# One-token attention with an MLP beside it: cache tiles of four heads on one load queue, folds on TensorE, and weights in the cache buffers

## Chip, cores, metric

The kernel runs on one core of one Trainium2 chip. The metric is the device time of one execution in microseconds, as the median of several executions. Where two kernels are compared by a ratio, it is the mean time of one kernel's fast runs over the mean time of the other's in the same rounds on the same chip, so it is not quite the ratio of the medians beside it.

## The reference

Eight requests each decode one token: a layer norm, attention of 32 heads over a cache of 4096 keys, and an MLP of the doubly normalised input; the sum of both and the input goes out.

```python
B, Sq, D = 8, 1, 576;  H, Sk, Dh = 32, 4096, 128;  F = 4608      # all bf16

q = (x @ wq).reshape(B, Sq, H, Dh).transpose(0, 2, 1, 3)
scores = einsum("bhqd,bhkd->bhqk", q, k_cache) * (Dh ** -0.5)
o = einsum("bhqk,bhkd->bhqd", softmax(scores), v_cache)
A = o.transpose(0, 2, 1, 3).reshape(B, Sq, H * Dh) @ wo

h = gelu(layernorm(x) @ w1 + b1)          # B_ref, x is already normalised once
out = x0 + A + h @ w2 + b2
```

The two caches are 268 MB each; every byte of them is read once and meets one multiply-add. The weights are 20 MB.

## The kernel before

The program is laid out in stages, each with its own memory pools: the query projection, then the MLP, then the attention loop, then the output projection. A pool that is closed gives its memory to the next one, so the cache buffers (`kv_pool`) partly lie where the MLP's weights lay.

```python
    wo_sb = const.tile([P, H, D], BF16, name="wo_sb")
    nc.gpsimd.dma_start(out=wo_sb, in_=A_wo.rearrange("(h p) d -> p h d", p=P))
    ...                                   # wq, layer norms, q8 = queries, qT = their transposes
    with tc.tile_pool(name="mlp_w", bufs=1) as mlp_w, ...:
        w1_sb = mlp_w.tile([P, NDC, F], BF16, name="w1_sb")        # 46 KB a partition
        w2_sb = mlp_w.tile([P, FC, D], BF16, name="w2_sb")         # 41 KB a partition
        b1T = mlp_w.tile([P, FC], BF16, name="b1T")
        nc.gpsimd.dma_start(out=b1T, in_=B_b1.rearrange("(c p) -> p c", p=P))
        ...                               # the whole MLP
```

The loop takes two heads of one request at a time. A head's 4096 keys lie as 128 partitions of 32 keys, 8 KB of contiguous memory each. K comes on the queue of SyncE and V on that of ScalarE, three buffers each. Twelve of the 32 key columns are transposed and scored on TensorE; the other 20 are multiplied by the broadcast query on VectorE and folded there from 128 products to 8 by a tree of additions. The values are 64 matmuls with a single moving column each.

```python
        for b in range(B):
            for hg in range(NHG):
                nc.sync.dma_start(
                    out=k_sb, in_=A_k_cache[b, h0:h0 + HG].rearrange("g (p c) d -> p g c d", p=P))
                nc.scalar.dma_start(
                    out=v_sb, in_=A_v_cache[b, h0:h0 + HG].rearrange("g (p c) d -> p g c d", p=P))
                ...
                        nc.tensor.matmul(tp[:, t * P:(t + 1) * P], lhsT=k_sb[:, g, c, :], rhs=ident[:, :], ...)
                        nc.scalar.activation(out=kT[:, g, blk, :], in_=tp[:, :], func=ACT.Copy)
                ...
                        nc.tensor.matmul(sc_ps[:, g, c:c + 1], lhsT=kT[...], rhs=qT[:, h, b:b + 1], ...)
                ...
                        nc.vector.tensor_tensor(out=prod[:, g, :, :], in0=k_sb[:, g, X:C, :], in1=qb_cur[...], op=ALU.mult)
                        while width > 8:  # 128 -> 64 -> 32 -> 16 -> 8
                            nc.vector.tensor_tensor(out=prod[:, g, :, 0:half], in0=..., in1=..., op=ALU.add)
                        nc.vector.tensor_reduce(out=sc_ps[:, g, X:C], in_=prod[:, g, :, 0:width], ...)
                ...
                    nc.scalar.activation(out=E[:, g, :], in_=sc_ps[:, g, :], func=ACT.Exp, accum_out=...)
                ...
                    for c in range(C):
                        nc.tensor.matmul(o_ps[:, g:g + 1], lhsT=v_sb[:, g, c, :], rhs=E[:, g, c:c + 1], ...)
```

The softmax here doesn't subtract the row's maximum and nothing guards it: scores larger than these inputs give would overflow.

## Time and profile before

| | before |
|---|---|
| median time, 13 runs | 1392.74 us (1391.15 to 1395.41) |
| span of the profiled run | 1389.7 us |
| first K load issued | 85.83 us |
| last K tile read | 1361.15 us |
| cache stream in between | 1275.3 us, 536.9 MB, 421 GB/s |
| mean rate over the span | 401 GB/s |
| TensorE's granted clock, mean | 0.52 |
| instructions | 33564 |

The lines of the profile are shown in the prediction. To read them: the rows of digits are 40 equal slices of the span, a digit being the busy share in tenths; `PEclk` is the clock that TensorE was granted, in tenths of full speed; `DMA` is the share for which the 16 DMA engines moved packets. A line of busy times by stage has the stretch, its length, busy time and number of instructions of PE, PEld, VectorE, ScalarE and POOL (PE is TensorE's matmuls, PEld its weight loads, POOL is GpSimd; SPq and ACTq, further down, are the queues of SyncE and ScalarE that issue loads), then granted clock, DMA share and GB/s. The question put to such a profile is which resource is full, when, and what happens in the slices where it is not.

### The profile page before, as it was taken

The page shows a single profiled execution, that of the slowest core. Times are in us where ns is not written, and L with a number is a line of the kernel's source. Part 1 is how long each engine was busy: PE and PEld are TensorE (multiplying, and loading weights), DVE is VectorE, ACT ScalarE, POOL GpSimd, SP SyncE. Part 2 cuts the span into 40 slices and gives each one's busy share as a digit, 9 for nine tenths or more (in the row PEclk, how much of TensorE's full clock was granted, in tenths as well). Part 3 has the DMA queues.
Part 4 walks back from the last instruction along what each step waited for, and adds up shares of the span by engine and source line. Part 5 has one row for each costly group of instructions (what it writes and reads, how often), then busy time and mean ns, then how long its engine had stood idle before and what let it go on. Part 6 is the DMA issues. An engine that isn't in the chain of part 4 may idle for free.

```text
span 1389.7 us, 33564 instructions
## 1 busy us (share of the span) xinstructions
PE 800.5 (58%) x14800; PEld 670.2 (48%) x14800; DVE 850.2 (61%) x1604; ACT 551.4 (40%) x1485; POOL 9.6 (1%) x17
## 2 busy tenths in 40 slices
PE   4645565746565556565556555655556555556566
PEld 1324454545454545454545454555445545445454
DVE  2026666666666676666675766666766666666663
ACT  2213343534344434443444443443435443434342
POOL 1100000000000000000000000000000000000000
PEclk9565555555555555555555555555555555555556
DMA  7859999999999999999999999999999999999991
GB/s 273 306 203 427 425 426 426 426 426 426 426 424 424 424 419 426 420 426 426 416 425 426 413 427 419 425 425 418 425 423 419 425 421 427 424 415 426 417 425 69
DMA packets 73458, 559.12 MB, mean 402 GB/s; under 512 B 4424, under 2 KB 4448, under 8 KB 6624
## 3 DMA queue, kind: packets, MB, share of 16 engines
q10 hardware_dynamic: 35472, 273.16, 47.2%
q1 hardware_dynamic: 34848, 268.46, 45.8%
q0 software_dynamic: 2992, 15.35, 3.1%
q8 instruction: 115, 1.88, 0.5%
q14 instruction: 31, 0.25, 0.0%
HBM read 556.95 MB, written 0.01 MB: 401 GB/s over the span
## 4 chain that ended last, share of the span: by engine, by line
DMA 63%; DVE 21%; PE 11%; ACT 3%; issue 1%; ACTq 1%; POOL 0%; DVEq 0%; SPq 0%
DMA k_sb<-in_A_k_cache_dram 60%; DVE prod L287 9%; DVE prod L278 9%; PE o_ps L308 6%; DMA b1T<-in_B_b_dram 2%; PE tp L260 2%; DVE sc_ps L294 2%; ACT kT L264 2%; DMA wq_sb<-in_A_wq_dram 1%; ACT E L302 1%; PE qps L142 1%; PE acc L336 1%; PE mlp_ps L200 1%; ACTq L242 1%; ACT O_sb L312 0%
## 5 line engine op out<-in xcount | busy, mean ns | idle before, releaser
L278 DVE TENSOR_TENSOR prod<-k_sb,qb_sb 128x2560 bf16<-128x2560 bf16 x256 | 370.4, 1489 | 444.9 <-DMA k_sb<-in_A_k_cache_dram 444.9
L308 PE MATMUL o_ps<-E,v_sb 128*128 128x1 bf16 x8192 | 236.3, 165 | 463.7 <-ACT E L302 463.7
L264 ACT ACTIVATE kT<-tp 128x512 bf16<-128x512 f32 x768 | 442.5, 596 | 117.2 <-PE tp L260 85.1
L308 PEld LDWEIGHTS <-v_sb 128*128 128x128 bf16 x8192 | 243.2, 105 | 488.7 <-issue 488.7
L260 PE MATMUL tp<-ident,k_sb 128*128 128x128 bf16 x3072 | 440.7, 302 | 63.7 <-ACT kT L264 31.8
L287 DVE TENSOR_TENSOR prod<-prod 128x1280 bf16<-128x1280 bf16 (+3 forms) x1024 | 401.4, 466 | 0.1
L260 PEld LDWEIGHTS <-k_sb 128*128 128x128 bf16 x3072 | 291.6, 130 | 99.2 <-issue 59.6
L302 ACT ACTIVATE E<-sc_ps 128x32 bf16<-128x32 f32 x256 | 48.1, 193 | 474.4 <-DVE sc_ps L294 474.4
L269 PEld LDWEIGHTS <-kT 128*128 128x128 bf16 x3072 | 171.0, 116 | 53.2 <-ACT kT L264 53.1
L269 PE MATMUL sc_ps<-qT,kT 128*128 128x1 bf16 x3072 | 173.0, 172 | 5.1 <-ACT kT L264 0.2
L294 DVE TENSOR_REDUCE sc_ps<-prod 128x20 f32<-128x160 bf16 x256 | 83.4, 326 | 6.1 <-PE sc_ps L269 1.7
L312 ACT ACTIVATE O_sb<-o_ps 128x2 f32<-128x2 f32 x128 | 22.3, 174 | 156.9 <-PE o_ps L308 156.9
L228 PE MATMUL qb_ps<-q,sel 8*128 8x512 bf16 x64 | 37.3, 583 | 20.7 <-ACT qb_sb L229 20.6
L229 ACT ACTIVATE qb_sb<-qb_ps 128x512 bf16<-128x512 f32 x64 | 38.4, 599 | 26.3 <-DVE prod L278 16.0
L302 ACT ACTIVATION_READ_ACCUMULATOR E<-sc_ps 128x1 f32 x256 | 47.7, 198 | 0.0
L142 PE MATMUL qps<-wq_sb,xT 128*8 128x512 bf16 (+1 forms) x40 | 13.9, 457 | 11.0 <-DMA wq_sb<-in_A_wq_dram 11.0
L179 DVE TENSOR_TENSOR x<-hT_ps,b1T 128x288 f32<-128x288 f32 x1 | 0.5, 458 | 29.1 <-DMA b1T<-in_B_b_dram 29.1
L200 PE MATMUL mlp_ps<-w_sb,hT_sb 128*8 128x512 bf16 x72 | 10.3, 309 | 10.2 <-DVE hT_sb L190 10.2
L172 PEld LDWEIGHTS <-w_sb 128*128 128x128 bf16 (+1 forms) x180 | 10.6, 106 | 6.6 <-issue 5.4
L150 DVE CAST qT<-tq 128x8 bf16<-128x8 f32 x32 | 4.1, 162 | 14.2 <-PE tq L149 14.0
L146 ACT ACTIVATE q<-qps 8x512 bf16<-8x512 f32 x8 | 4.7, 587 | 20.2 <-PE qps L142 20.2
L172 PE MATMUL hT_ps<-yT,w_sb 128*128 128x8 bf16 (+1 forms) x180 | 12.0, 176 | 0.3 <-DVE qT L150 0.3
(56 smaller groups left out, 65.5 us busy)
## 6 DMA issues: line engine op xcount, KB each, us to landing
k_sb<-in_A_k_cache_dram SPq DMA_DIRECT2D x128, 2048.0 KB, 18.9
v_sb<-in_A_v_cache_dram ACTq DMA_DIRECT2D x128, 2048.0 KB, 17.1
w_sb<-in_B_w_dram POOLq DMA_DIRECT2D x1, 5184.0 KB, 30.8
wo_sb<-in_A_wo_dram POOLq DMA_DIRECT2D x1, 4608.0 KB, 26.9
w_sb<-in_B_w_dram POOLq DMA_DIRECT2D x4, 1152.0 KB, 9.0
wq_sb<-in_A_wq_dram ACTq DMA_DIRECT2D x4, 1024.0 KB, 9.7
w_sb<-in_B_w_dram POOLq DMA_DIRECT2D x1, 576.0 KB, 17.3
wq_sb<-in_A_wq_dram ACTq DMA_DIRECT2D x1, 512.0 KB, 18.0
```

What stands on the lines that cost most here:

```text
L142: nc.tensor.matmul(qps[:, :nn], lhsT=xT[:dn, ci, :], rhs=wq_sb[:dn, ci, n0:n0 + nn], start=(ci == 0), stop=(ci == NDC - 1),)
L200: nc.tensor.matmul(mlp_ps2[:, n0:n0 + nn], lhsT=hT_sb[:, fc, :], rhs=w2_sb[:, fc, n0:n0 + nn], start=(fc == 0), stop=(fc == FC - 1),)
L228: nc.tensor.matmul(qb_ps[:, :nn], lhsT=sel[:, b, :], rhs=q8[:, n0:n0 + nn], start=True, stop=True)
L229: nc.scalar.activation(out=qb_sb[:, n0:n0 + nn], in_=qb_ps[:, :nn], func=ACT.Copy)
L260: nc.tensor.matmul(tp[:, t * P:(t + 1) * P], lhsT=k_sb[:, g, c, :], rhs=ident[:, :], start=True, stop=True,)
L264: nc.scalar.activation(out=kT[:, g, blk, :], in_=tp[:, :], func=ACT.Copy)
L269: nc.tensor.matmul(sc_ps[:, g, c:c + 1], lhsT=kT[:, g, blk, t * P:(t + 1) * P], rhs=qT[:, h, b:b + 1], start=True, stop=True,)
L278: nc.vector.tensor_tensor(out=prod[:, g, :, :], in0=k_sb[:, g, X:C, :], in1=qb_cur[:, h * Dh:(h + 1) * Dh].unsqueeze(1).to_broadcast([P, R ...
L287: nc.vector.tensor_tensor(out=prod[:, g, :, 0:half], in0=prod[:, g, :, 0:half], in1=prod[:, g, :, half:width], op=ALU.add,)
L294: nc.vector.tensor_reduce(out=sc_ps[:, g, X:C], in_=prod[:, g, :, 0:width], axis=mybir.AxisListType.X, op=ALU.add,)
L302: nc.scalar.activation(out=E[:, g, :], in_=sc_ps[:, g, :], func=ACT.Exp, accum_out=Epart[:, h, b:b + 1],)
L308: nc.tensor.matmul(o_ps[:, g:g + 1], lhsT=v_sb[:, g, c, :], rhs=E[:, g, c:c + 1], start=(c == 0), stop=(c == C - 1),)
```

## The change

The intent is to let the transfer of the caches run from the first microseconds to the last and to keep all compute behind it. Tiles hold four heads of one request, 32 partitions a head, so each partition takes 32 KB of contiguous memory. All loads go on SyncE's queue through four buffers of 32 KB a partition; wq and w1 use these buffers before the stream, wo and w2 after it. VectorE multiplies all keys, TensorE folds the products against an identity matrix, and the values are matmuls of 512 moving columns. The order of all engines is fixed by hand. The core of the diff, cut:

```diff
+    ctx.enter_context(tc.manual_schedule(
+        engines={ENG.PE, ENG.DVE, ENG.Activation, ENG.SP, ENG.Pool}))
     const = ctx.enter_context(tc.tile_pool(name="const", bufs=1))
+    kv = ctx.enter_context(tc.tile_pool(name="kv", bufs=4))
...
+    wq_sb = kv.tile([P, WN * 2, HQ], BF16, name="wq_a", tag="kv")
+    wq_sb2 = kv.tile([P, WN, HQ], BF16, name="wq_b", tag="kv")
...
+    w1_sb = kv.tile([P, WN * 2, HF], BF16, name="w1_a", tag="kv")
+    w1_sb2 = kv.tile([P, WN, HF], BF16, name="w1_b", tag="kv")
...
+    def load_kv(cache, hg, b, name):
+        t = kv.tile([P, C, Dh], BF16, name=name, tag="kv")
+        nc.sync.dma_start(
+            out=t[:].rearrange("p c d -> p (c d)"),
+            in_=cache[b, hg * G:(hg + 1) * G].rearrange("g (p c) d -> (g p) (c d)", p=QP),
+        )
+        return t
...
-                nc.sync.dma_start(
-                    out=k_sb, in_=A_k_cache[b, h0:h0 + HG].rearrange("g (p c) d -> p g c d", p=P)
-                )
-                nc.scalar.dma_start(
-                    out=v_sb, in_=A_v_cache[b, h0:h0 + HG].rearrange("g (p c) d -> p g c d", p=P)
-                )
...
+        for n in range(NCB):
+            prod = prp.tile([P, CB, Dh], BF16, name="prod", tag="prod")
+            nc.vector.tensor_tensor(
+                out=prod, in0=k[:, n * CB:(n + 1) * CB, :],
+                in1=qb[:, v, b, h2].unsqueeze(1).to_broadcast([P, CB, Dh]), op=ALU.mult)
+            ps = ps_s.tile([P, CB, DL], FP32, name="s_ps", tag="s")
+            nd = Dh // DL
+            for d in range(nd):
                 nc.tensor.matmul(
...
+                    ps, lhsT=ident, rhs=prod[:, :, d * DL:(d + 1) * DL],
+                    start=(d == 0), stop=(d == nd - 1))
...
+        for j in range(J):
+            nc.tensor.matmul(
+                ps, lhsT=e[:, j], rhs=v[:, 4 * j:4 * j + 4, :], start=(j == 0), stop=(j == J - 1))
...
+        sc = scores(i, k_t)
+        if pend is not None:
+            gather(*pend)
...
+            softmax_last(i, sc)
+            values_last(i, v_t)
...
+    cuts = [(0, 0, R), (1, 0, R // 2), (1, R // 2, R - 3), (1, R - 3, R)]
+    for v, r0, r1 in cuts:
+        nc.sync.dma_start(out=w2_sb[v][:, r0:r1, :], in_=w2_v[v, :, r0:r1, :])
...
-        fin = fin_sb.tile([B, D], BF16, name="fin")
-        nc.vector.tensor_tensor(out=fin, in0=acc, in1=mlpx_sb, op=ALU.add)
+    fin = const.tile([B, D], BF16, name="fin")
+    nc.vector.tensor_copy(out=fin, in_=acc[:, :D])
```

## The prediction

> **What bounds the kernel now.** I read the page's slices first, then the chain of waits, the busy times by stage, the waits of the DMA-issuing queue, and the timeline of the end.
>
> The slices show a core whose DMA engines are full in 36 of 40 slices, at about 425 GB/s, while no compute engine is above seven tenths in the middle. The clock line says that TensorE is granted half of its speed almost throughout.
>
> ```profile
> span 1389.7 us, 33564 instructions
> DVE  2026666666666676666675766666766666666663
> PEclk9565555555555555555555555555555555555556
> DMA  7859999999999999999999999999999999999991
> GB/s 273 306 203 427 425 426 426 426 426 426 426 424 424 424 419 426 420 426 426 416 425 426 413 427 419 425 425 418 425 423 419 425 421 427 424 415 426 417 425 69
> q8 instruction: 115, 1.88, 0.5%
> HBM read 556.95 MB, written 0.01 MB: 401 GB/s over the span
> DMA k_sb<-in_A_k_cache_dram 60%; DVE prod L287 9%; DVE prod L278 9%; PE o_ps L308 6%; DMA b1T<-in_B_b_dram 2%; PE tp L260 2%; DVE sc_ps L294 2%; ACT kT L264 2%; DMA wq_sb<-in_A_wq_dram 1%; ACT E L302 1%; PE qps L142 1%; PE acc L336 1%; PE mlp_ps L200 1%; ACTq L242 1%; ACT O_sb L312 0%
> ```
>
> The chain runs through VectorE work for 20%, but that is a path through a loaded pipe, not the bound: the busy times by stage (busy time and count per engine, clock, DMA share, GB/s) have the DMA share at 1.01 over the whole cache stream and under it only at the two ends.
>
> ```profile
> 30.00:40.00 10.00, 7.75 (x46) 3.48 (x46) 3.42 (x27) 5.22 (x9) 6.54 (x8) 0.82 0.52 191
> 60.00:80.00 20.00, 9.83 (x104) 6.28 (x104) 3.02 (x7) 0.44 (x1) 0.00 (x0) 0.57 0.21 67
> 100.00:1350.00 1250.00, 723.46 (x14046) 627.43 (x14044) 817.59 (x1509) 522.05 (x1423) 0.00 (x0) 0.50 1.01 423
> 1360.00:1370.00 10.00, 7.67 (x145) 6.75 (x143) 7.00 (x14) 5.78 (x15) 0.00 (x0) 0.50 0.14 57
> 1370.00:1380.00 10.00, 6.78 (x83) 3.73 (x83) 2.42 (x3) 0.64 (x5) 0.00 (x0) 0.50 0.01 2
> ```
>
> What holds the first K load back shows in the waits of the issuing queue and in the timeline, where that load is issued only at 85.83 us; the last K tile is read at 1361.15 us and the output projection closes the run.
>
> ```profile
> SPq L239 <- DMA w_sb<-in_B_w_dram: 65.8, 1, 65.8
> SPq L239 <- DVE mlpx_sb L206: 15.1, 1, 15.1
> 85.83 1.42 SPq L239 DMA_DIRECT2D k_sb<-in_A_k_cache_dram  x3
> 1361.15 1.49 DVE L278 TENSOR_TENSOR prod<-k_sb,qb_sb 128x2560 bf16<-128x2560 bf16 x1 [3.30 <-DMA k_sb<-in_A_k_cache_dram]
> 1376.13 10.50 PE L336 MATMUL acc<-wo_sb,On 128*8 128x512 bf16 x64 [2.53 <-DVE On L326]
> ```
>
> So the span is 85.8 us of setup, 1275.3 us of stream and 28.6 us of tail. The caches are 2 x 8 x 32 x 4096 x 128 x 2 bytes = 536.9 MB, which makes the stream 421 GB/s. The four weight matrices are 20.1 MB, or 47 us at 425 GB/s: the setup spends about 39 us more on them than their bytes need, because the cache buffers wait for the MLP to finish, and the tail has an idle DMA.
>
> **What the Trainium skill says.** "DMA: Bandwidth & Descriptors", section "Bandwidth", gives 425 GB/s for a 16 MB load by one core and a ceiling of 435.2 GB/s. The trace agrees: 426 to 427 in the clean slices. The section "Issuing engines are not separate DMA queues" says that several issuing engines save only issue time; this case's trace has two queues in the stream and cannot confirm it, and the change relies on it. "TensorE: Matmul & The Clock Gate", Part 1, says that a dense stream of some 4 us doubles the clock. The trace agrees at the end of the run: the output projection's pairs of 512 and 64 columns come every 0.48 us until 1381.3 us, then 21 pairs take 5.02 us, 0.239 us each. That is 0.83 and 0.415 ns a column. "SBUF — State Buffer", section "Door 1: The DMA port swizzle", gives SBUF lines of 16 bytes and full bandwidth within one. No operand of the kernel before is read by TensorE in strided runs of 16 bytes, so the trace does not test it.
>
> **The change, part by part.**
>
> Setup. It removes the pool that made the caches wait for the MLP. The weights wq (4.72 MB) and w1 (5.31 MB) now sit in the same four buffers of 32 KB a partition as the cache tiles; wo and w2 move to the end. Ten MB at 425 GB/s are 23.6 us, from about 2 us on: the weights have landed at about 26 us. To follow without a gap, K of tile 0 needs the first wq buffer free by then. The normalised input is ready at 6.8 us in the trace; 18 tiny copies, one wide copy, nine transposes and two masks are added, so I estimate its spread form at 13 us. The first 24 query matmuls then take 24 x about 0.25 us (the trace's dense query groups: five in 1.26 us at full clock), so the buffer is free at 19 us. V follows. K of tile 1 needs the first w1 buffer; the 162 hidden matmuls of 16 columns cost 0.11 us each by the trace's weight loads (106 ns), 18 us after about 24 us, and the buffer frees near 36 to 40 us, before the 45.7 us at which tile 0 has landed. I see no gap. First cache byte at 26 us instead of 86.
>
> Stream. A tile is now 4 heads with 32 rows each, 4.19 MB of K and as much of V: 64 tiles, 19.7 us each at 426 GB/s. Rows are 32 KB of contiguous memory instead of 8 KB, all on one queue. VectorE loses the add tree and keeps two multiplies of 8192 elements and two reductions of 512. The slope between 1280 and 2560 elements is (1489 - 819)/1280 = 0.523 ns for one, so a multiply is 1489 + 5632 x 0.523 = 4.44 us; with some 0.7 us a reduction, 10.3 us a tile. TensorE loses the transposes and gets 32 matmuls against the identity that fold 128 products to 8, and 32 for the values, each 512 columns: 32768 x 0.415 = 13.6 us at full clock, 27.3 us at half. ScalarE has four exponentials at about 0.4 us with their accumulator reads and two small copies. K is released after its two multiplies, 8.9 us after it lands; its buffer is wanted again 29.5 us after landing. V is released about 4.4 + 7 + 4 + 7 = 22.5 us after K has landed, which is 12.7 us after its own landing, and has 29.5 us too. At full clock all of it hides behind the transfer. Executed TensorE instructions fall to a third, which should remove most of the 1.88 MB of instruction fetches.
>
> Rate. The pace of clean stretches in the trace (multiply starts at 603.95, 613.71 and 623.55 us: 9.8 us for 4.19 MB) is 428 GB/s and the mean 421; every 95 us or so a stretch of 10 to 20 us falls to between 391 and 415. I take 426 for the new kernel, since there is less fetching and rows are longer: 536.9 MB / 426 = 1260 us.
>
> Tail. After the last V byte come wo in 1152-byte rows (estimate 350 GB/s, 13.5 us) and w2 in long rows (12.5 us). The last tile's values are computed meanwhile: 128 narrow matmuls at 29 ns, since 64 of these took 1.85 us before, done some 10.5 us after V. 68 pairs of 512 and 64 columns at 0.24 us are 16 us and follow the weights; after the last piece only three pairs remain. Receipt 2, pairs 0.8, copy 0.7, output 2.4 us: the tail is about 32 us, a little longer than before, but it now carries 10 MB.
>
> Sum: 2 + 23.6 + 1260 + 32 = 1317.6 us of span. The measured times lie 1.8 to 3.4 us above the span; with the small chance of a better rate I say 1317 us, 5.5% less than 1393.
>
> **Rivals.**
> First, TensorE becomes the bound. At half clock it needs 27.3 us a tile: 64 x 27.3 + 60 gives 1800 us. For it: the clock line is 5 although TensorE was busy 58%. Against it: those matmuls had 1 or 128 columns; the new ones are dense, and a TensorE that falls behind has no idle time left and so warms, as the end of this trace shows. A milder form: the 16-byte strided reads run at half rate, 32 x 0.213 = 6.8 us more, 20.4 us a tile plus 1 us of gathers; then 64 x 21.5 + 60 = 1436 us, slower. I give both together 5%.
> Second, one queue with four large buffers does not keep 16 engines full; a hole of 1 us a tile costs 64 us and leaves 1380 us, the same. Against it: two to four loads should be pending at any time by the release times above. 4%.
> Third, the stream keeps its mean of 421 GB/s because the dips are not instruction fetches: 1275 us of stream, 1333 in all. 20%.
> Fourth, long rows bring it to 431 GB/s: 1246 us, 1303 in all. 20%.
> Fifth, the setup has a gap because a weight buffer frees late: each late microsecond adds one; I allow 10 us, 1327.
>
> **Range and chances.** The third and the fourth rival with a few microseconds at the ends give 1302 to 1336 us. Under 1365 us is faster by over 2%: 0.93. Within 2%: 0.03, a hole in the queue. Slower: 0.04, TensorE.
>
> **What would show each step.** Right: DMA share at 1.0 from the second slice to the last but one, first K issue before 26 us, PEclk at 8 or more in most slices, multiplies near 4.44 us, matmuls of both kinds spaced some 0.21 us, fewer packets on q8, a tail of some 32 us with full DMA for 25 of them. Wrong: VectorE no longer waiting for K but for TensorE (TensorE is the bound); GB/s with regular holes while the issuing queue waits on a matmul or multiply (late release); 421 GB/s with the same dips although q8 is small (the dips are something else).

## The result

The changed kernel took 1311.16 us in the median of 8 runs (1311.02 to 1312.0), against 1392.74 us before. The ratio is 0.9416, with a 95% interval from 0.9407 to 0.9426: 5.8% less.

The page of the kernel after, the lines that answer to those of before:

```profile
span 1309.3 us, 11800 instructions
DVE  2645545545545545544554554654654553654550
PEclk9799999999989999999998999989998989989998
DMA  9999999999999999999999999999999999999997
GB/s 402 431 430 430 431 430 431 431 432 430 431 432 432 431 431 431 431 430 430 431 429 431 430 432 432 432 432 432 431 429 431 430 431 432 429 431 432 430 418 274
q8 instruction: 40, 0.66, 0.2%
HBM read 556.94 MB, written 0.01 MB: 425 GB/s over the span
DMA k<-in_A_k_cache_dram 73%; DVE prod L281 21%; PE acc L268 1%; PE qps L213 1%; PE hT_ps L242 1%; PE s_ps L287 0%; PE o_last L329 0%; ACT e_last L321 0%; DMA prod<-in_A_x_dram 0%; DVE prod L181 0%; PE tp L185 0%; ACT L156 0%; DVE par L177 0%; DVE prod L158 0%; ACT q L220 0%
```

The `DMA` row is nine in 39 of 40 slices. The holes of the first three slices are gone, and the plateau stands at 429 to 432 GB/s where it was 413 to 427. VectorE is at half, and the digit of TensorE's clock is 9 or 8 in all slices but one.

The busy times by stage of the kernel after, with the columns as explained above:

```profile
0.00:10.00 10.00, 0.47 (x8) 0.47 (x9) 4.90 (x27) 1.58 (x2) 3.75 (x15) 1.00 0.81 314
10.00:20.00 10.00, 6.69 (x33) 2.86 (x33) 3.60 (x13) 0.29 (x1) 0.00 (x0) 1.00 1.01 432
20.00:30.00 10.00, 9.28 (x102) 6.26 (x101) 1.28 (x2) 3.44 (x5) 0.00 (x0) 0.89 1.06 452
100.00:1250.00 1150.00, 965.23 (x4309) 419.68 (x4308) 595.77 (x251) 144.73 (x602) 0.00 (x0) 0.94 1.00 431
1290.00:1300.00 10.00, 10.00 (x78) 4.65 (x76) 0.66 (x2) 0.00 (x0) 0.00 (x0) 0.96 0.92 384
1300.00:1310.00 10.00, 6.33 (x52) 2.90 (x50) 0.75 (x1) 0.00 (x0) 0.00 (x0) 1.00 0.13 50
```

And its timeline at the two ends (start, duration, engine, line, operation):

```profile
21.22 0.33 SPq L125 DMA_DIRECT2D k<-in_A_k_cache_dram  x1
...
32.44 0.33 SPq L125 DMA_DIRECT2D k<-in_A_k_cache_dram  x1
...
1268.24 8.76 DVE L281 TENSOR_TENSOR prod<-k,qb 128x8192 bf16<-128x8192 bf16 x2 [6.28 <-DMA k<-in_A_k_cache_dram]
...
1284.00 3.56 PE L329 MATMUL o_last<-e_last,v 128*128 128x4 bf16 x128 [2.35 <-ACT e_last L321]
...
1297.35 8.98 PE L268 MATMUL acc<-w,hT_sb 128*8 128x512 bf16 x72
1306.37 0.75 DVE L408 CAST fin<-acc 8x576 bf16<-8x576 f32 x1 [12.07 <-PE acc L268]
```

The load of the first cache tile is issued while w1 is still on its way, so the transfer never pauses: the first 10.0 MB, the weights, have passed after 26.0 us (314, 432 and 452 GB/s in the first three stretches of 10 us). The last V load was issued at 1251.8 us; the median landing of a V load is 24.7 us after issue, so it landed at about 1276.5 us. The span divides like this:

| | before | after | difference | predicted difference |
|---|---|---|---|---|
| setup, until the caches move | 85.8 us | 26.0 us | -59.8 | -60.2 |
| cache stream | 1275.3 us | 1250.5 us | -24.8 | -15.3 |
| tail | 28.6 us | 32.8 us | +4.2 | +3.4 |
| span | 1389.7 us | 1309.3 us | -80.4 | -72.1 |

The stream after is 536.9 MB in 1250.5 us, or 429 GB/s. Its first and last microseconds are read from cumulated rates and a median landing, so they are good to 1 or 2 us. The stream before is counted to the last K tile read, at 1361.15 us; the line from 1360 us on in the prediction (57 GB/s for 10 us, 0.6 MB) shows that the V loads had then ended too, so the two streams compare.

### The profile page after: what moved, and what is told of

Same layout as the page of the kernel before. It is cut to its first block, busy times and chain, and to the rows that moved or that the text cites. A ratio compares the mean times of both kernels' runs of the same rounds, so it can differ in the third digit from the quotient of the medians.

```text
span 1309.3 us, 11800 instructions
## 1 busy us (share of the span) xinstructions
PE 1085.0 (83%) x5150; PEld 480.2 (37%) x5150; DVE 661.9 (51%) x321; ACT 163.0 (12%) x662; POOL 3.7 (0%) x15
## 2 busy tenths in 40 slices
DMA packets 24089, 557.71 MB, mean 426 GB/s; under 512 B 2259, under 2 KB 6372, under 8 KB 6630
## 4 chain that ended last, share of the span: by engine, by line
DMA 74%; DVE 22%; PE 3%; ACT 0%; issue 0%; DVEq 0%; ACTq 0%
DMA k<-in_A_k_cache_dram 73%; DVE prod L281 21%; PE acc L268 1%; PE qps L213 1%; PE hT_ps L242 1%; PE s_ps L287 0%; PE o_last L329 0%; ACT e_last L321 0%; DMA prod<-in_A_x_dram 0%; DVE prod L181 0%; PE tp L185 0%; ACT L156 0%; DVE par L177 0%; DVE prod L158 0%; ACT q L220 0%
## 5 line engine op out<-in xcount | busy, mean ns | idle before, releaser
L281 DVE TENSOR_TENSOR prod<-k,qb 128x8192 bf16<-128x8192 bf16 x128 | 560.7, 4422 | 387.5 <-DMA k<-in_A_k_cache_dram 387.5
L308 PE MATMUL o_ps<-v,ebd 128*16 128x512 bf16 x2016 | 507.1, 416 | 118.2 <-ACT ebd L300 118.2
L287 PE MATMUL s_ps<-prod,ident 128*128 128x512 bf16 x2048 | 465.4, 381 | 87.2 <-DVE prod L281 87.0
L308 PEld LDWEIGHTS <-ebd 128*16 128x16 bf16 x2016 | 189.5, 96 | 410.3 <-ACT ebd L300 124.3
L287 PEld LDWEIGHTS <-ident 128*128 128x128 bf16 x2048 | 198.1, 98 | 349.9 <-issue 131.7
L292 DVE TENSOR_REDUCE sc<-s_ps 128x64 f32<-128x512 f32 x128 | 88.1, 689 | 200.3 <-PE s_ps L287 200.3
L300 ACT ACTIVATE ebd<-sc 32x128 bf16<-32x128 f32 x252 | 77.3, 307 | 17.9 <-DVE sc L292 14.9
L337 PEld LDWEIGHTS oT<-selc,ob 16*128 16x128 f32 x504 | 60.7, 186 | 26.7 <-issue 26.7
L337 PE MATMUL oT<-selc,ob 16*128 16x4 f32 x504 | 66.2, 250 | 0.0
L300 ACT ACTIVATION_READ_ACCUMULATOR ebd<-sc 32x1 f32 x252 | 46.3, 184 | 0.0
## 6 DMA issues: line engine op xcount, KB each, us to landing
v<-in_A_v_cache_dram SPq DMA_DIRECT2D x64, 4096.0 KB, 24.7
```

The costliest lines, as they stand in the source:

```text
L281: nc.vector.tensor_tensor(out=prod, in0=k[:, n * CB:(n + 1) * CB, :], in1=qb[:, v, b, h2].unsqueeze(1).to_broadcast([P, CB, Dh]), op=ALU.mult)
L287: nc.tensor.matmul(ps, lhsT=ident, rhs=prod[:, :, d * DL:(d + 1) * DL], start=(d == 0), stop=(d == nd - 1))
L292: nc.vector.tensor_reduce(out=sc[:, n * CB:(n + 1) * CB], in_=ps, axis=AX.X, op=ALU.add)
L300: nc.scalar.activation(out=e[rows, :, g, :], in_=sc[rows, :].rearrange("p (j c) -> p j c", c=4), func=ACT.Exp, scale=scale, accum_out=Ep[r ...
L308: nc.tensor.matmul(ps, lhsT=e[:, j], rhs=v[:, 4 * j:4 * j + 4, :], start=(j == 0), stop=(j == J - 1))
L337: nc.tensor.matmul(ps, lhsT=ob[:, c, :], rhs=selc[:, c, :], start=(c == 0), stop=(c == 3))
```

## Experiments

Three questions were put to the chip. What made the stream faster than 426 GB/s: longer rows, fewer instructions to fetch, or one queue in place of two? How near is TensorE to being the bound? And can the ends be improved?

### 8 KB pieces in place of 32 KB rows (rows8k)

```diff
-        t = kv.tile([P, C, Dh], BF16, name=name, tag="kv")
+        t = kv.tile([P, U, n + 16], BF16, name=name, tag="kv")     # U = 4, n = 4096 elements
         nc.sync.dma_start(
-            out=t[:].rearrange("p c d -> p (c d)"), ...
+            out=t[:, :, 0:n], ...
```

The 16 spare elements (32 bytes) after each piece keep the transfer from being one run of 32 KB. Nothing else differs but the views by which the tile is read.

> The changed kernel with one thing undone: each cache tile still comes in one load on one queue, but its rows land in four pieces of 8 KB with a gap of 32 bytes between them, so each transfer moves 8 KB as in the kernel before and not 32 KB. Theory of row length (a fixed cost per packet, worked out as about 4.4 ns from clean stretches at 427.3 GB/s with 8 KB and 432.0 GB/s with 32 KB): the clean rate falls to 427 GB/s, the time rises by 13 to 15 us to about 1325 us, with some 65 thousand more packets... of 8 KB for the caches. Theory that only instruction fetches or the number of queues made the stream faster: no change, 1311 us within 2.

Measured: 1335.48 us, ratio to before 0.9589 (0.9573 to 0.9605), 24.3 us more than the changed kernel. The page counts 73241 packets in place of 24089, that is 49152 more (the expectation's number was wrong). The busy times of its stream:

```profile
100.00:1250.00 1150.00, 952.50 (x4226) 414.19 (x4225) 585.99 (x246) 142.35 (x592) 0.00 (x0) 0.94 1.01 423
```

The stream fell from 431 to 423 GB/s with the same instructions on the same queue, so the shape of the transfer does matter, and more than expected: 24.3 us for 3072 more packets on each of the 16 DMA engines are 7.9 ns a packet. It also fell below the 426 GB/s that 8 KB packets had in the clean slices of the kernel before, which row length alone cannot explain.

### 2 KB pieces (rows2k)

The same edit with U = 16.

> The same with sixteen pieces of 2 KB a row. Row length with 4.4 ns a packet: 75.6 + 4.4 = 80.0 ns for 2 KB on one of 16 engines, 410 GB/s, some 67 us more, about 1379 us. If short rows cost more than a fixed time per packet, still slower; if row length is without effect, 1311 us.

Measured: 1434.74 us, ratio 1.0302 (1.0286 to 1.0317). This is slower than the kernel before.

```profile
100.00:1250.00 1150.00, 897.48 (x3915) 387.45 (x3914) 546.07 (x226) 131.17 (x543) 0.00 (x0) 0.93 1.05 392
```

123.6 us more for 15360 more packets an engine are 8.0 ns a packet, about the same as with 8 KB. So the cost goes with the number of packets, as the theory says, but it is nearly twice the 4.4 ns that were worked out from two kernels that differ in more than row length. The later runs show that two costs are in it. Note the DMA share: 1.05 while it moves 392 GB/s. A share of 1 does not say that bytes move at the best rate.

### The bias load moved to the front of the kernel before (before_b1early)

```diff
-        b1T = mlp_w.tile([P, FC], BF16, name="b1T")
-        nc.gpsimd.dma_start(out=b1T, in_=B_b1.rearrange("(c p) -> p c", p=P))
...
+    b1T = const.tile([P, FC], BF16, name="b1T")
+    nc.gpsimd.dma_start(out=b1T, in_=B_b1.rearrange("(c p) -> p c", p=P))
     wo_sb = const.tile([P, H, D], BF16, name="wo_sb")
```

> The kernel before with its first-layer bias load (4608 single elements of 2 bytes, which landed 32 us after its issue and ended the wait of the MLP) moved to the start of the program, ahead of the weights. The MLP then waits for its second weight matrix alone (landed at about 67 us in place of the bias at 70 us, or sooner without the small packets in front): the first cache load is issued 3 to 15 us earlier and the time falls by as much, to between 1378 and 1390 us. If the bias was not what held the MLP: 1393 us.

Measured: 1405.78 us, 14.6 us slower than before (ratio 1.0101, 1.0085 to 1.0116): a miss. Its timeline and busy times:

```profile
82.84 16.18 SPq L239 DMA_DIRECT2D k_sb<-in_A_k_cache_dram  x4
```

```profile
100.00:1350.00 1250.00, 714.22 (x13845) 619.16 (x13846) 806.41 (x1487) 514.97 (x1403) 0.00 (x0) 0.50 1.01 418
```

The setup did what was expected of it, at the low end: the first cache load left at 82.84 in place of 85.83 us. But the stream, whose code was not touched, ran at 418 in place of 423 GB/s. What did move were the addresses. The built programs tell where each buffer starts in its partition: in the kernel before, K and V buffers start on multiples of 256 bytes (72960, 122112, ...); the small bias tile ahead of them shifted all by 96 bytes (73056, 122208, ...). The buffers of the changed kernel start 96 bytes past a multiple of 256 too (48736, 147040, ...). "DMA: Bandwidth & Descriptors" of the Trainium skill, section "How a descriptor splits into AXI transactions", says that a descriptor which does not start on 256 bytes has a first transaction from the boundary below, whose unused bytes still cost beats. That gave the next two runs. They change the other kernel; no run repeats the early bias with its buffers back on a multiple of 256, so for this run the cause is argued from them.

### The changed kernel with its buffers moved by 160 bytes (aligned)

```diff
     const = ctx.enter_context(tc.tile_pool(name="const", bufs=1))
+    align = const.tile([P, 80], BF16, name="align")                # never used
```

> The changed kernel with 160 unused bytes ahead of its buffers, nothing else. As built, its cache buffers start 96 bytes past a multiple of 256 in each partition, while those of the kernel before start on a multiple; moving the buffers of the kernel before by 96 bytes (which the run with the early bias did as a side effect) went with a stream of 418 in place of 423 GB/s. If the start matters by a fixed time per packet (2.4 to 4.6 ns, estimated from 8 KB packets at 420, 423 and 426 GB/s), 1024 packets per engine make 2.5 to 4.7 us: 1306.5 to 1309 us, faster than both kernels. If the early bias slowed its stream by something else: 1311 us.

Measured: 1306.37 us (1306.21 to 1306.97), ratio 0.9383 (0.937 to 0.9396): 4.8 us less than the changed kernel, whose interval begins at 0.9407. It beats both kernels.

```profile
100.00:1250.00 1150.00, 976.09 (x4328) 422.77 (x4327) 600.30 (x252) 145.21 (x603) 0.00 (x0) 0.94 1.00 433
```

The buffers' start in SBUF (the on-chip memory) is worth 2 GB/s with 32 KB packets: 4.8 us over 1024 packets an engine are 4.7 ns each.

### 8 KB pieces, each on a multiple of 256 bytes (rows8k_al)

The edit of the first experiment with 128 spare elements in place of 16, and the 160 bytes in front.

> The run with 8 KB pieces again, now with every piece starting on a multiple of 256 bytes (gaps of 256 in place of 32 bytes). If the start matters: the stream returns to about the 426 GB/s that 8 KB packets had in the kernel before, 1324 to 1328 us, and what remains over 1311 is row length. If it does not: 1335 us as with the gaps of 32 bytes. If row length were nothing but alignment: 1311 us or less.

Measured: 1321.34 us, ratio 0.9489 (0.9476 to 0.9502).

```profile
100.00:1250.00 1150.00, 962.23 (x4273) 417.80 (x4272) 594.03 (x249) 142.86 (x593) 0.00 (x0) 0.94 1.01 428
```

Here both causes come apart. Between the two aligned kernels, 32 KB and 8 KB packets differ by 15.0 us, 4.9 ns for each further packet on an engine: row length. Between the two kernels with 8 KB pieces the start differs by 14.1 us, 3.5 ns for each of 4096 packets on an engine: alignment. (With gaps of 32 bytes one piece in eight starts on a multiple of 256 by chance, so this is a mean over all.) The 7.9 ns of rows8k hold both; for 2 KB pieces no run takes them apart. Nor was any multiple but 256 tried: whether 64 or 128 bytes would do, and whether the page's extra transaction is the mechanism, stays open. The changed kernel won about 15 us by its rows and gave 4.8 us back by where its buffers start.

### One queue for the kernel before (before_oneq)

```diff
-                nc.scalar.dma_start(
+                nc.sync.dma_start(
                     out=v_sb, in_=A_v_cache[b, h0:h0 + HG].rearrange("g (p c) d -> p g c d", p=P)
```

> The kernel before with its V loads issued from SyncE as well, so that one queue carries the stream; nothing else is changed. If one queue in place of two was part of the gain: the stream speeds up by up to 10 us, 1383 us. If it is row length and instruction fetches: 1393 us within 3.

Measured: 1387.63 us, ratio 0.9976 (0.9959 to 0.9993), 3.5 us less than the 1391.18 us of before in the same rounds. The theory of queues allowed up to 10 us; the other one expected no more than 3 us either way, and the measurement lies just outside, with an interval (1.0 to 5.7 us by the ratio) that reaches into both. The slices decide more than the time. Its page, and the busy times of its stream:

```profile
GB/s 273 308 187 426 426 426 426 426 426 426 426 426 426 426 425 427 425 426 426 426 426 426 426 426 426 425 426 426 425 427 424 426 426 425 427 421 425 419 410 84
100.00:1250.00 1150.00, 699.94 (x12996) 625.84 (x12997) 758.16 (x1386) 476.02 (x1318) 0.00 (x0) 0.50 1.01 426
```

The dips that the prediction took for instruction fetches, slices of 413 to 420, are gone from the middle, though this kernel runs the same 14800 matmuls and 14800 weight loads and its instruction queue moves the same 1.88 MB. So fetches alone do not make them. They belong to the arrangement with K and V on two queues; by which mechanism, and whether fetches have a part in it there, no run here shows. From 100 to 1250 us the rate rose from 423 to 426 GB/s, more than the time tells: near the end this kernel's stream is thinner, 225 GB/s from 1350 to 1360 us against 392 in the kernel before.

### V on ScalarE's queue in the changed kernel (v_act)

```diff
     def load_kv(cache, hg, b, name):
+        q = nc.scalar if name == "v" else nc.sync
         t = kv.tile([P, C, Dh], BF16, name=name, tag="kv")
-        nc.sync.dma_start(
+        q.dma_start(
```

> The changed kernel with the V loads issued from ScalarE, so that two queues carry the stream as in the kernel before. If one queue is part of the gain in rate, the stream slows by up to 10 us (1321). If the queues share the same engines and nothing else, 1311 us within 3; a small loss can come from ScalarE waiting with a load issue for a V buffer ahead of its exponentials.

Measured: 1314.82 us, ratio 0.9445 (0.9431 to 0.9459), 3.7 us more than with one queue. Who waited for whom in it (us in all, times, longest):

```profile
PE o_ps L309 <- DMA v<-in_A_v_cache_dram: 141.1, 46, 8.6
```

From 100 to 1250 us the stream's rate is the same 431 GB/s as with one queue. What changed is the order of landing: with two queues V lands 29.9 us after its issue in the median, where it was 24.7, and K 26.6 in place of 30.0; TensorE waits for V 46 times, which it never did before this edit. The last tile's narrow value matmuls then start at 1286.8 in place of 1284.0 us, and the end moves with them. One queue is worth some 3.5 us of the time in both kernels, by order in this one.

### More instructions (moreinst)

```diff
         if i + 1 < len(tiles):
+            tiny(100)          # 100 matmuls 128x128 with one moving column
             e = softmax(i, sc)
```

> The changed kernel with 100 pairs of a weight load and a one-column matmul added per tile (12600 more instructions on TensorE, 2.9 us of its time a tile, in the gap where it waits for the exponentials and a little beyond). Theory of instruction fetches (a dip of the transfer rate of about 1.4 us for each 2048 TensorE instructions: 14 dips before, 5 after): about 6 more dips and 8 to 9 us, 1320 us, and the instruction queue moves about 1.5 MB in place of 0.66. Theory that the dips are something periodic on the chip or in memory: 1311 to 1313 us, five dips as now.

Measured: 1356.26 us (1347.03 to 1356.83), ratio 0.9722 (0.9691 to 0.9754): far over both expectations, for a reason that neither had. One tile from its timeline:

```profile
602.74 7.08 PE L295 MATMUL s_ps<-prod,ident 128*128 128x512 bf16 x32
...
610.73 2.72 PE L203 MATMUL tiny<-tiny_w 128*128 128x1 bf16 x100
...
613.38 9.89 PE L316 MATMUL o_ps<-v,ebd 128*16 128x512 bf16 x32
...
623.21 7.08 PE L295 MATMUL s_ps<-prod,ident 128*128 128x512 bf16 x32
```

A tile takes 20.47 us, over the 19.5 us of the transfer, and TensorE is busy 98% of the span. The narrow matmuls themselves cost 2.72 us; but after them the 32 value matmuls take 9.89 us, where they take 7.07 us at full clock (fill32), because the first of them come 0.427 us apart, the spacing of half clock. The mean granted clock is 0.86 in place of 0.94. So the time says nothing on fetches, but it shows the first rival of the prediction at work, and, with fill8 below, that one-column matmuls count for little when TensorE's clock is granted, however busy the engine looks. (In the kernel before, TensorE was busy 58% of the span, with matmuls of 1 and of 128 columns, at a clock of 0.52; idle time has its part there.) On fetches the start of the run does say something. Before TensorE held up the loads, the stream ran at almost the rate of the changed kernel with more than twice the instructions on TensorE: from 100 to 450 us 430 GB/s with 3128 matmuls, against 431 GB/s with 1344.

### Idle matmuls of 512 columns: 8 and 32 a tile (fill8, fill32)

```diff
         if i + 1 < len(tiles):
+            filler(8)          # or 32
             e = softmax(i, sc)
```

> The changed kernel with 8 idle matmuls of 512 columns per tile (1.7 us at full clock) where TensorE waits for the exponentials. Theory that TensorE is off the path: its granted clock rises from 0.94 towards 1.0 and the time stays at 1311 us within 2. A theory in which the clock matters: faster than 1311.

Measured: 1312.68 us, ratio 0.9431 (0.9417 to 0.9445), which overlaps the interval of the changed kernel. The mean clock rose from 0.937 to 0.986, and the time did not fall. Clock on an engine off the path was worth nothing here.

> The same with 32 idle matmuls, 6.9 us a tile. TensorE's work of about 16.3 us a tile becomes about 22.6 us, over the 19.45 us of the transfer: TensorE is the bound, the time is about 1480 to 1510 us, and the DMA share falls below 0.9. If TensorE had more spare time than I count (over 10 us), still 1311.

Measured in a single run, state unknown: 1477.98 us, 2 us under the expected range, clock 0.99. The DMA share from 100 to 1250 us was 0.91, where less than 0.9 had been expected. Its timeline:

```profile
704.65 7.07 PE L308 MATMUL o_ps<-v,ebd 128*16 128x512 bf16 x32
...
711.65 7.08 PE L287 MATMUL s_ps<-prod,ident 128*128 128x512 bf16 x32
...
719.65 7.08 PE L357 MATMUL fill<-warm,ident 128*128 128x512 bf16 x31
```

The tile takes 22.0 us, three blocks of 7.07 us and 0.9 us of gathers (the small matmuls that pick a tile's results out of the blocks), and TensorE is the bound. The blocks also answer the question on strided reads: the folds read runs of 16 bytes, the values whole rows, and both take 7.07 to 7.08 us for 32 matmuls, 0.221 us each. This agrees with the 16-byte lines of "SBUF — State Buffer".

### Three buffers in place of four (bufs3)

```diff
-    kv = ctx.enter_context(tc.tile_pool(name="kv", bufs=4))
+    kv = ctx.enter_context(tc.tile_pool(name="kv", bufs=3))
```

> The changed kernel with three cache buffers in place of four. By the release times (V's buffer is free some 24 us after its K tile landed, and with three buffers is wanted at 29 us) the stream does not notice; the start loses 2 to 5 us because the last third of w1 must wait for a query weight buffer: 1313 to 1317 us. The rival that few large buffers leave holes: at least 1 us a tile more, 1375 us or more.

Measured: 1314.32 us, ratio 0.9447 (0.9431 to 0.9463), 3.2 us more, as expected. The stream ran at 430 GB/s; w1's last third was issued at 21.34 us in place of the first microseconds. The rival of too few buffers is refuted for this layout with one buffer to spare; 32 KB a partition could be used otherwise.

### Half of wo ahead of the last V tile (tail)

```diff
             k_n = load_kv(A_k_cache, *tiles[i + 1], "k")
+            if i + 2 == len(tiles):
+                wo_sb = kv.tile([P, H // 2, D], BF16, name="wo_a", tag="kv")
+                nc.sync.dma_start(out=wo_sb, in_=wo_v[:, :H // 2, :])
             v_n = load_kv(A_v_cache, *tiles[i + 1], "v")
...
             softmax_last(i, sc)
+            for h in range(H // 2):
+                accumulate(On[:, h // G, h % G, :], wo_sb[:, h, :])
             values_last(i, v_t)
```

> An attempt to beat both: the first half of wo is loaded ahead of the last V tile and its 16 heads are accumulated while TensorE waits for the last exponentials, so that TensorE no longer closes the run 2 us after the last weights have landed. Expected: 1 to 3 us less than the changed kernel, about 1309 us; the last weight piece lands at 1301 to 1304 us as now and TensorE ends 1 us after it. If the end is bound by the transfer alone already: 1311.

Measured: 1311.4 us, ratio 0.9421 (0.9407 to 0.9435): no gain. Its timeline:

```profile
1281.80 4.08 PE L268 MATMUL acc<-wo_a,On 128*8 128x512 bf16 x32
...
1291.11 6.53 PE L268 MATMUL acc<-wo_b,On 128*8 128x512 bf16 x32 [1.67 <-DMA wo_b<-in_A_wo_dram]
...
1306.50 0.75 DVE L409 CAST fin<-acc 8x576 bf16<-8x576 f32 x1 [16.26 <-PE acc L268]
```

The first half did fill the wait, at full clock (4.08 us in place of 5.67). But the second half then had to wait 1.67 us for its weights and ran at half clock for most of its 6.53 us, after the 128 four-column value matmuls and that wait, where it took 4.08 us in the changed kernel. The gain was spent 10 us later, and VectorE's last copy starts at 1306.50 us as against 1306.37. The expectation that transfer alone would close the run was wrong too: TensorE still does.

## Why the prediction was right

The predicted 1317 us was 0.4% over the measured 1311.16, inside the range, and the mechanism was the one predicted: the whole stream is transfer, and the setup no longer stands in front of it.

**Setup.** Predicted first cache byte at 26 us, read at 26.0. Inside, two terms were off and cancelled or did not matter. The spread query input was ready at 10.6 us, not 13, but the query matmuls stood behind the second layer norm's transposes in TensorE's order and began at 14.17 us. Eight of them came at half clock, 0.427 us apart, so the first buffer was free at 21.2, not 19 us. It was still 5 us before it was needed. The hidden layer freed its first buffer at 32.4 us, not 36 to 40.

**Compute behind the stream.** The groups of the kernel after (busy time, mean of one, idle before and releaser):

```profile
L281 DVE TENSOR_TENSOR prod<-k,qb 128x8192 bf16<-128x8192 bf16 x128 | 560.7, 4422 | 387.5 <-DMA k<-in_A_k_cache_dram 387.5
L308 PE MATMUL o_ps<-v,ebd 128*16 128x512 bf16 x2016 | 507.1, 416 | 118.2 <-ACT ebd L300 118.2
L287 PE MATMUL s_ps<-prod,ident 128*128 128x512 bf16 x2048 | 465.4, 381 | 87.2 <-DVE prod L281 87.0
```

The multiply was predicted at 4.44 us and took 4.422. VectorE waits for K, 387.5 us in all, which was named as the mark of a right prediction. The clock is 0.94. But the margin was judged too large: TensorE was counted with 13.6 us of a 19.7 us tile, and is busy 83% of the span; 2.7 us of narrow matmuls were enough to make it the bound (moreinst). Two blocks take 14.1 us at full clock (fill32) and the gathers, which the 13.6 us leave out, 1.05 us. The rest shows in the mean of 416 ns for the value matmuls against 381 for the folds: after many of the waits for the exponentials some of them run at half clock (six or seven of 32 in the block that starts at 1264.12 us, none in that at 1244.69 us).

**Stream.** This is the term that was mis-sized, by 9.5 us: 426 GB/s predicted (1260 us), 429 measured (1250.5 us), 431 in the middle. The fourth rival, long rows at 431 GB/s, came nearest to what happened, and it had been given 20%. For a better rate the prediction named fewer instruction fetches first and longer rows second. The first step failed: the dips it rested on vanish with one queue and unchanged instructions (before_oneq). By the third rival's reasoning the stream should then have stayed at 421 GB/s; that the dips went all the same, with the second queue, was luck. Row length is shown as the larger cause, 15.0 us, less 4.8 us for the buffers' start (aligned, rows8k_al). One queue gave 3.5 us of the whole time (before_oneq), and by the rates more. The means of 10 us windows from 100 to 1250 us are 423.4 GB/s before, 425.7 with one queue (before_oneq), 427.5 with the changed kernel's aligned 8 KB rows, 432.7 with its aligned 32 KB rows and 431.0 as changed. For 536.9 MB these would be 1268, 1261, 1256, 1241 and 1246 us, an estimate: some 7 us for the queue, 5 us for what is left between the two kernels, 15 us for the rows, and 5 us lost by the start. For the 5 us left no run gives the cause. The fetches moved 1.22 MB less, which at 430 GB/s would be 2.8 us if they compete for the same engines, an estimate; loads of 4 MB in place of 2 MB are another candidate.

**Tail.** Predicted 32 us, measured 32.8. But what closes the run is TensorE, not the last weight piece: after the last values end at 1287.5 us it works through 68 pairs almost without a pause, the first seven at half clock, until 1306.3 us, while the DMA share is down to 0.13 after 1300 us. The prediction had three pairs left after the last piece. By its own numbers, 10.5 us to the last values and 16 us of pairs, TensorE needed 26.5 us after the last V byte and the weights 26.0 us; the two were never added up, and that the sum came out within 1 us is in part luck. For wo the prediction guessed 350 GB/s and named no number that it came from; from 1276 to 1288 us the loads ran at 332.

**Rivals.** TensorE as the bound and holes from few buffers did not occur. The first was shown to be near: 2.7 us of narrow matmuls a tile bring it on (moreinst). The prediction's argument against it, that a TensorE that falls behind has no idle time left and so warms, held for dense matmuls (fill32, where TensorE is the bound at a clock of 0.99) and failed with narrow ones among them: in moreinst it was busy for all of the 100 us from 500 us on and was granted 0.83. (The milder form of this rival adds up to 21.4 us a tile and 1430 us, not 21.5 and 1436; it did not occur.) The second is not near: three buffers cost 3.2 us (bufs3), and fewer were not tried.

## What to carry to other kernels

When the DMA is full, look first at the slices where it is not: three quarters of this gain (59.8 of 80.4 us of the span, read from the two traces; no run undoes this part alone) came from a setup whose buffers shared memory with work that had to end first. Then look at the packets: a full DMA share hides a fixed cost per packet, so load the longest contiguous rows that the layout allows and try the buffers on multiples of 256 bytes; one unused tile of 160 bytes a partition was worth 4.8 us here. Engines behind the stream need spare time, not speed, but narrow matmuls eat it twice, once by themselves and once by the clock of what follows.

## What the Trainium skill lacked or had wrong

- "DMA: Bandwidth & Descriptors", section "How a descriptor splits into AXI transactions", speaks of where a descriptor starts and of bytes fetched there, and does not say that a load's start in SBUF counts. Here a start 96 bytes past a multiple of 256 cost 4.7 ns per 32 KB packet (1311.16 against 1306.37 us), and starts mostly off it cost 3.5 ns per 8 KB packet (1335.48 against 1321.34 us). No page says that a kernel's first small tile can shift all its buffers.
- The same page, section "Why small descriptors are slow (HBM only)", gives a fixed cost per packet but calls joining descriptors worth it only at 256 bytes or less; it does not say that longer rows still gain far above that. Between aligned packets of 8 and 32 KB lay 15.0 us of 1306, 4.9 ns a packet; unaligned packets of 2 KB brought the stream down to 392 GB/s.
- The same page, section "Issuing engines are not separate DMA queues", says that several issuing engines save only issue time. The changed kernel's rate agrees (431 GB/s with one queue and with two); the kernel before ran at 423 GB/s with two and 426 with one, and the order of landing changes: V on a second queue made TensorE wait for it 141 us in all and the changed kernel 3.7 us slower.
- "TensorE: Matmul & The Clock Gate", Part 1, says that activity frees the clock, not which. 100 one-column matmuls a tile took the mean clock from 0.94 to 0.86 while TensorE was busy 98% of the span (moreinst); 8 matmuls of 512 columns in the same place took it to 0.99 (fill8).
